# Turning the third token group by transposing transfers instead of TensorE, with w3's last tile loaded once

## The chip, the cores and the metric

The kernel runs on one core of a Trainium2 chip. The metric is the device time of one execution in microseconds, lower is better. The engines are named as in the profile: PE (TensorE's matmuls; PEld is its weight loads), DVE (VectorE), ACT (ScalarE), POOL (GpSimd) and SP (SyncE, which here issues nearly every DMA). "L453" is line 453 of the kernel.

## The reference

The input `x` has 2048 tokens of 448 channels. Two branches are added to it:

```python
xn  = layernorm(x)
out = x + A(xn) + B(xn)

def A(x):                      # spectral filter
    X = rfft2(x) * (w_r + 1j * w_i)
    return irfft2(X)

def B(x):                      # token shift, then MLP
    h  = gelu(layernorm(x) @ w1)                # w1: 448 x 448
    hs = concat(shift(h[:, 0:112], +1), shift(h[:, 112:224], -1),
                shift(h[:, 224:336], +2), shift(h[:, 336:448], -2)) @ w2
    x1 = x + hs
    h2 = gelu(layernorm(x1) @ w3) @ w4          # w3: 448 x 1792, w4: 1792 x 448
    return x1 + h2
```

## The kernel before

**Numbers.** Every matrix product is made in float16 from operands that are split into a high and a low half (`hi`, `lo = x - hi`), in three passes: hi·hi, lo·hi, hi·lo. The products with 448 channels contract over four tiles of 128, 128, 128 and 64 channels; the last, half-filled tile holds the high half in rows 0 to 63 and the low half in rows 64 to 127, so a split `x` has seven tiles (`xT`, 7 x 512 columns). For the same reason the last 64 rows of `w3` stand twice in `w3raw[:, 3]`, in partitions 0 to 63 and 64 to 127. The weights are scaled before splitting by a power of two that is found on chip: ACT squares and sums the raw weights (`squares`, L239), and `powers` (L245) adds the sums on DVE, adds them over the partitions by a small float32 matmul with ones (L254, "the power matmul") and makes the scale on DVE.

**Tokens.** Sixteen rows b of 128 tokens (token 16a + b stands in partition a of row b) form four groups, `GRP = [[14, 15, 0, 1], [2, 3, 4, 5], [6, 7, 8, 9], [10, 11, 12, 13]]`. "The third group" is group 2, rows 6 to 9. A shift of the tokens is then a change of row, so the w2 product of row b reads h of rows b-1, b+1, b-2 and b+2, one for each of the channel quarters k = 0 to 3.

**Stages of branch B, for each group.**

1. The group is normalised in place (`norm1`, L327).
2. It is turned, channels into partitions. Groups 0 to 2: 16 transposes by PE into PSUM (`turn_pe`, L398, L403), and from there a copy by ACT (L413) and a subtraction by DVE (L414) for each of four tiles make `xT` (`turn_copy`, `T1`). Group 3: `turn` (L819) splits each row into halves in SBUF first (ACT L825, DVE L826 and L827) and has SP transpose the row by one DMA (L828).
3. `w1_unit(g, i)` (L465) multiplies by w1 (L453, 11 matmuls for each row), applies the gelu on ACT (L474), splits the result into halves (ACT L475, DVE L476) and has SP transpose it into `hT` (L479), one DMA for each row.
4. `w2_mm(b, ks)` (L485) makes the w2 product of row b for the channel quarters `ks`, three matmuls for each (L497), and `w2_tile` finishes a row and adds it to x (DVE L504).
5. `ln2` (L507) normalises again and transposes by DMA into `x2all`, which lies in the memory `x2mem`.

The MLP follows: `front` (L424: w3; the gelu; halves in `hf`) and `back` (L772: w4) for 8 groups of 256 tokens and 7 pairs of feature tiles. It runs in the order of low priority, as filler between everything else; branch A (the transforms) is interleaved with it. `w3_split` (L831) makes the halves of w3 in eight pieces, four for each half of the features.

**Order of the work.** The program is written in the order of priority. A scheduler with a model of the times builds each engine's queue from that: of the instructions that are ready in its model, the one of highest priority goes next. `with behind(key)` adds an edge: what is issued inside comes behind the named instructions in the queue of the same engine. It is an order and no wait. Each engine, SP too, works off its queue in order. The keys in this change: `("a2")` the copies that turn group 2, `("a3")` the same for group 3, `(g, i)` the two halves of h of a unit, `("h", g, i)` its transposing DMA, `("w2", b)` the last w2 matmul issued for row b, `("p3")` the power matmul of w3, `("T", g)` the PE transposes of a group.

**Memory.** `bank(tag, ...)` gives one of two PSUM banks for each of the four tags mm, acc, tr and sp; a new user waits until the bank's last one has been read. `stage(name, n, side)` gives one of two SBUF buffers: side 0 holds first w1 and later ln2's rows 0 and 1, side 1 holds w2, then group 3's halves.

Of the kernel before, what the change touches and what calls it, by code (L numbers as in the profile page):

```python
# [13 lines left out]
F16 = mybir.dt.float16  # L14
I32 = mybir.dt.int32
AF = mybir.ActivationFunctionType
ALU = mybir.AluOpType
# [17 lines left out]
PIN = [("a3",), ("a3",), ("a3",), ("a3",)]  # L35
WMAX = [(1, 4), (1, 5), (1, 6), (2, 0), (2, 1), (2, 2), (2, 3), (2, 4)]
LATE = [(2, 2), (2, 3), (2, 4), (2, 5)]
# [84 lines left out]
def body(tc, nc, x, wf, w1, w2, w3, w4, c_g, c_n, c_small, out):  # L122
# [89 lines left out]
    def load_w3(ts):  # L212
        for t in ts:
            if t < 3:
                SY.dma_start(w3raw[:, t], w3[128 * t:128 * t + 128])
            else:
                for h in range(2):
                    SY.dma_start(w3raw[64 * h:64 * h + 64, 3], w3[384:448])

    load_w3([0, 1])  # L220
    load_x(3)
    load_w3([2])
    x2mem = pw.tile([128, 9 * F], F16, name="x2mem")
# [20 lines left out]

    def powers(m, n, key, tag="acc", mid=None):  # L245

        t = pc.tile([128, 1], F32, name=f"pt{key}")
        i = V.tensor_reduce(out=t, in_=m[:, :n + 1], axis=AX.X, op=ALU.add)
        after["t" + key] = (i.ins,)
        if mid:  # L250
            with behind("t" + key):
                mid()
        pm = bank(tag, f"pm{key}") if isinstance(tag, str) else tag
        i = T.matmul(pm[:, 0:1], ones, t, start=True, stop=True)  # L254
        after["p" + key] = (i.ins,)
        e = pc.tile([128, 3], I32, name=f"pe{key}")
        V.tensor_scalar(out=e[:, 0:1], in0=pm.bitcast(I32)[:, 0:1], scalar1=1, scalar2=0x7F800000,
                        op0=ALU.logical_shift_right, op1=ALU.bitwise_and)
        V.tensor_scalar(out=e[:, 1:2], in0=e[:, 0:1], scalar1=-1, scalar2=185 << 23, op0=ALU.mult, op1=ALU.add)
        i = V.tensor_scalar(out=e[:, 2:3], in0=e[:, 0:1], scalar1=1, scalar2=69 << 23, op0=ALU.mult, op1=ALU.add)  # L260
        after["s" + key] = (i.ins,)
        return e.bitcast(F32)[:, 1:2], e.bitcast(F32)[:, 2:3]
# [202 lines left out]
    def w1_unit(g, i, pm=None):  # L465
        if pm is None:
            pm = bank(("tr" if g == 1 else "mm", "acc")[i // 2], f"pw1_{g}{i}")
            w1_in(g, [(i, pm)], range(4))
        c = CS[GRP[g][i]]
        pm = pm[:, :D]  # L470
        pv_ = pm.rearrange("p (k n) -> p k n", k=4)
        h = hs_buf[c % (HS if g == 3 else HS + 2)]
        with behind(0, i - 2) if g == 0 and i > 1 else contextlib.nullcontext():
            A.activation(out=pm, in_=pm, func=AF.Gelu_apprx_tanh, scale=gsc[:, c:c + 1])  # L474
        u = A.activation(out=h[:, 0, :, 0:112], in_=pv_, func=AF.Copy, scale=h1)  # L475
        v = V.scalar_tensor_tensor(out=h[:, 1, :, 0:112], in0=pv_, scalar=h1, in1=h[:, 0, :, 0:112],  # L476
                                   op0=ALU.mult, op1=ALU.subtract)
        o = h_at(g, i)
        d = SY.dma_start_transpose(out=hT[g][:, :, o:o + 128], in_=h.rearrange("p i k n -> p (i k n)"))  # L479
        after[g, i] = u.ins, v.ins  # L480
        after["h", g, i] = (d.ins,)
# [3 lines left out]
    def w2_mm(b, ks):  # L485
        if b not in w2b:
            w2b[b] = bank("sp", f"pw2_{b}")
        for k in ks:
# [330 lines left out]
    def turn(g):  # L819

        xTs[g] = p1.tile([128, 7, 512], F16, tag="xT", bufs=2, name=f"xT{g}")
        y = stage(f"x{g}", 8 * D, 1, F16).rearrange("p (i n) -> p i n", i=4)
        for i, b in enumerate(GRP[g]):
# [4 lines left out]
            d = SY.dma_start_transpose(out=xTs[g][:, :, 128 * i:128 * i + 128], in_=h)  # L828
        after["t", g], after[f"a{g}"] = (d.ins,), (u.ins, v.ins)

# [85 lines left out]
    h_alloc(1)  # L916
    for k in range(4):
        w1_unit(1, k)
    for b in range(2):
        w2_mm(b, (2, 0))  # L920
    after["T", 2] = after["w2", 1]
    T1(2)
    with behind("h", 1, 3):
        load_w3([3])
    with behind("w2p"):
        n1[0][2]()
        n1[1][2]()
        for f in n1[2][:3]:
            f()
    for b in range(2):  # L930
        with behind("T", 2):
            w2_tile(b, (1, 3))
# [3 lines left out]
    with behind("w2", 1):  # L936
        for k in range(4):
            w1_unit(2, k)
    for k in range(4):
        with behind(*(("a2",), ("a2",), (2, 0), (2, 1))[k]):  # L940
            squares(m3[:, k:k + 1], w3raw[:, k])
    s3, r3 = powers(m3, 4, "3", "mm")
    h3 = pc.tile([128, 1], F32, name="h3")
    V.tensor_scalar(out=h3, in0=s3, scalar1=2.0 ** -5, scalar2=None, op0=ALU.mult)
    for b in range(2, 4):
        w2_tile(b)
    turn(3)
# [6 lines left out]
    for b in range(4, 8):  # L954
        w2_tile(b)
        with behind(*PIN[b - 4]):
            w3_split(2 * b - 8)
            w3_split(2 * b - 7)
            for i in (2 * b - 10, 2 * b - 9):
                if i >= 0:  # L960
                    squares(m4[:, i:i + 1], flat(w4raw[:, 2 * i:2 * i + 2]), junk4)
# [114 lines left out]
```

## Time and profile before

| | |
|---|---|
| median of 3 runs | 413.18 us (413.17 to 413.48) |
| the profiled execution's own time | 413.19 us |
| its span, first to last instruction | 411.4 us |
| PE busy | 406.0 us (99%) |
| DVE, ACT, POOL busy | 294.4, 247.7, 114.6 us |
| granted TensorE clock | 0.999 |
| PE transposes (L403) | 48 in all, 16 for the third group, from 33.01 to 34.76 us |
| group 3's transposing transfers (L828) | 4, landing 3.0 us after issue (median) |

The profile is of one execution. In a timeline row the columns are the start in us, how long it took in us, the engine, the line, the operation, what is written and read, the shape and the number of instructions merged into the row; in square brackets, if at all, the idle time before and what ended it. Matmuls overlap, so the time of a run of matmuls is read from its start to the start of the next one. A row of the groups has the busy time in us and the mean of one in ns behind the bar. In the windows, each stretch has the PE, PEld, DVE, ACT and POOL busy time, then the clock, the busy share of the DMA engines and the GB/s that they moved.

### The profile page before, as it was taken

Reading aid. Unit: us, or ns where it says so; the run is one execution under the profiler, and the core shown is the slowest. Engines: PE = TensorE matmul, PEld = TensorE weight load, DVE = VectorE, ACT = ScalarE, POOL = GpSimd, SP = SyncE. Lnnn points to the kernel's source line nnn. Section 1 sums busy time; section 2 is a strip of 40 time slices with the busy share of each in tenths; the row PEclk is TensorE's granted clock in tenths of the full one; section 3 lists DMA queues with packets and bytes.
Section 4 is the critical chain, followed back from the end, with each engine's and each line's share of the span. In section 5 each row is a group of like instructions: output and inputs, shape, how many; then the busy total and the mean of one; then the engine's idle time right before and its main releaser. Section 6 shows DMA issues by size and latency. Waiting matters only on the chain.

```text
span 411.4 us, 8535 instructions
## 1 busy us (share of the span) xinstructions
PE 406.0 (99%) x3314; PEld 290.1 (71%) x3314; DVE 294.4 (72%) x638; ACT 247.7 (60%) x427; POOL 114.6 (28%) x205
## 2 busy tenths in 40 slices
PE   8999999999999999999999999999999999999996
PEld 3655555666667877776887888777776776677885
DVE  5988999897644758863689889875776787667122
ACT  4697979964638766862678888873343434342321
POOL 2987810011217746400031121211212221121000
PEclk9999999999999999999999999999999999999999
DMA  8979499806811383437056655610000213233001
GB/s 279 365 219 202 96 175 324 192 2 142 173 47 45 91 274 132 120 84 165 13 141 178 154 142 143 170 56 2 2 0 2 69 50 107 69 94 130 24 0 46
DMA packets 53496, 48.53 MB, mean 118 GB/s; under 512 B 37600, under 2 KB 48480, under 8 KB 53456
## 3 DMA queue, kind: packets, MB, share of 16 engines
q1 hardware_dynamic: 53456, 47.99, 43.5%
q8 instruction: 26, 0.43, 0.4%
q14 instruction: 14, 0.11, 0.1%
HBM read 35.52 MB, written 3.67 MB: 95 GB/s over the span
## 4 chain that ended last, share of the span: by engine, by line
PE 93%; DVE 3%; DMA 2%; ACT 1%; POOL 1%; issue 0%
PE pw L424 33%; PE acc L772 31%; PE pw L497 8%; PE pw L453 6%; PE pu L693 3%; PE ps L590 3%; PE pp L647 2%; PE pe L713 2%; PE px L664 2%; PE py L735 2%; DMA h<-x2mem 1%; DMA xt<-x 1%; DVE sta L312 1%; PE pta L403 1%; DVE xT L414 0%; DVE xt L352 0%
## 5 line engine op out<-in xcount | busy, mean ns | idle before, releaser
L424 PE MATMUL pw<-x2mem,w3p 128*128 128x256 f16 x1232 | 149.6, 273 | 0.0
L772 PE MATMUL acc<-w4p,hf 128*128 128x448 f16 (+1 forms) x714 | 138.0, 341 | 0.0
L424 PEld LDWEIGHTS <-w3p 128*128 128x128 f16 x1232 | 118.6, 98 | 19.4
L772 PEld LDWEIGHTS <-hf 128*128 128x128 f16 x714 | 69.4, 98 | 48.3 <-DVE hf L753 0.3
L749 ACT ACTIVATE pw<-pw,pe 128x512 f32<-128x512 f32 x56 | 36.7, 656 | 64.6 <-PE pw L424 63.4
L753 DVE SCALAR_TENSOR_TENSOR hf<-pw,h,hf 128x512 f16<-128x512 f32 x56 | 41.9, 749 | 43.6 <-ACT hf L752 43.3
L497 PE MATMUL pw<-w2p,h 112*128 112x448 f16 x192 | 39.4, 352 | 0.1
L752 ACT ACTIVATE hf<-pw,h 128x512 f16<-128x512 f32 x56 | 38.4, 685 | 1.2
L674 POOL TENSOR_TENSOR z<-te 128x450 f32<-128x450 f32 x16 | 16.0, 1003 | 73.0 <-DVE te L672 69.2
L453 PE MATMUL pw<-w1p,xT 128*128 128x448 f16 x176 | 35.1, 352 | 0.3 <-ACT xT L413 0.3
L720 POOL TENSOR_TENSOR e<-e 128x226 f32<-128x226 f32 x16 | 11.5, 721 | 77.8 <-ACT e L717 74.6
L497 PEld LDWEIGHTS <-h 112*128 112x128 f16 x192 | 18.6, 98 | 16.2 <-DMA h<-x2mem 0.5
L453 PEld LDWEIGHTS <-xT 128*128 128x128 f16 x176 | 17.1, 99 | 15.9 <-ACT xT L413 0.5
L654 ACT ACTIVATE pf<-pp 64x450 f16<-64x450 f32 x32 | 17.4, 543 | 16.7 <-DVE pf L655 8.3
L717 ACT ACTIVATE e<-pe 128x452 f32<-128x452 f32 x16 | 8.8, 548 | 26.4 <-PE pe L713 26.4
L655 DVE TENSOR_TENSOR pf<-pp,pf 64x450 f16<-64x450 f32 x32 | 19.9, 622 | 5.9 <-ACT pf L654 5.6
L570 POOL TENSOR_TENSOR xr<-xf 128x452 f32<-128x452 f32 x8 | 8.9, 1115 | 32.0 <-issue 27.6
L669 ACT ACTIVATE te<-px 64x450 f32<-64x450 f32 x32 | 17.3, 539 | 0.5
L728 DVE TENSOR_TENSOR vh<-e,vh 128x448 f16<-128x448 f32 x16 | 10.0, 625 | 9.7 <-ACT vh L727 9.7
L573 POOL TENSOR_TENSOR f<-xr 128x452 f32<-128x452 f32 x16 | 16.1, 1030 | 0.6
L581 DVE TENSOR_TENSOR xh<-f,xh 128x452 f16<-128x452 f32 x16 | 12.7, 833 | 5.0 <-ACT xh L580 5.0
L722 DVE TENSOR_TENSOR e<-e 128x113 f32<-128x113 f32 x16 | 9.9, 618 | 7.8 <-POOL e L720 7.8
(172 smaller groups left out, 600.5 us busy)
## 6 DMA issues: line engine op xcount, KB each, us to landing
wc<-wf SPq DMA_DIRECT2D x32, 225.0 KB, 3.6
wl<-wf SPq DMA_DIRECT2D x8, 450.0 KB, 3.7
xf<-x SPq DMA_DIRECT2D x8, 448.0 KB, 3.4
xt<-x SPq DMA_DIRECT2D x3, 896.0 KB, 11.1
w3raw<-w SPq DMA_DIRECT2D x3, 896.0 KB, 14.6
xr<-x SPq DMA_DIRECT2D x12, 224.0 KB, 2.6
out<-xr SPq DMA_DIRECT2D x12, 224.0 KB, 1.9
gn<-c_g SPq DMA_DIRECT2D x16, 128.0 KB, 3.2
```

Of the source, the lines that this page charges most:

```text
L424: T.matmul(ps_out, wp[:, wi + t, cols], xT[:, xi + t, tok], start=t == 0 and wi + xi == 0, stop=t == 3 and wi == 4)
L453: m = T.matmul(pm[:, :D], xTs[g][:, xi + t, 128 * i:128 * i + 128], w1p[:, wi + t], start=t == 0 and p == 0, stop=t == 3 and p == 2)
L497: m = T.matmul(w2b[b][:, :D], hT[g][:112, 4 * hi + k, o:o + 128], w2p[:, wi, k], start=k == 2 and hi + wi == 0, stop=k == 3 and hi == 1)
L573: P.tensor_tensor(out=f[:, :, k:k + 2].rearrange("p b s d -> p s b d"), in0=u[:, :, 0], in1=u[:, :, 1], op=op)
L654: A.activation(out=hi, in_=src, func=AF.Copy)
L655: V.tensor_tensor(out=lo, in0=src, in1=hi, op=ALU.subtract)
L669: i = A.activation(out=e[64 * h:64 * h + 64], in_=px_[64 - 64 * h:128 - 64 * h, :2 * DF], func=AF.Copy)
L674: P.tensor_tensor(out=z, in0=t[:, 0], in1=t[:, 1], op=ALU.add)
L749: A.activation(out=pm, in_=pm, func=AF.Gelu_apprx_tanh, scale=r3)
L752: i = A.activation(out=h[:, 0], in_=pm, func=AF.Copy, scale=h3)
L753: j = V.scalar_tensor_tensor(out=h[:, 1], in0=pm, scalar=h3, in1=h[:, 0], op0=ALU.mult, op1=ALU.subtract)
L772: m = T.matmul(to, h[:, hi, o:o + 128], w4p[0][:, wi, f, r], start=f == 0 and n == 0, stop=f == 13 and n == 2)
```

## The change

- Group 2 is turned as group 3 is: `turn(2)` stands between the first and the second w1 unit of group 1, and the 16 PE transposes with their copies are gone. Its halves use stage side 0. The halves of the units (1, 2) and (1, 3) come behind its copies on ACT and DVE.
- Of the w2 products, rows 0, 1, 2 (quarters 2 and 0) and row 3 (quarter 2) now stand ahead of the rest. PSUM: the w1 units of group 2 use tags tr and acc, the w2 products of rows 2 and 3 use mm, and the power matmul uses sp.
- w3's last 64 rows are loaded once, right behind the third tile in the opening loads; a second DMA, in SP's queue behind the transposition of h of unit (2, 0), copies them on chip to partitions 64 to 127.
- The squares of w3 come earlier: three behind the halves of unit (1, 3), the fourth behind those of unit (2, 0), the fourth on 64 partitions only. The power matmul is put right behind the last w1 matmul of group 2, and the rest of rows 2 and 3 of the w2 product behind it.
- `w3_split` also comes behind the halves of unit (2, 3). One of branch A's eight maxima (`WMAX`, used at L605) moves behind another piece of the MLP.

```diff
-WMAX = [(1, 4), (1, 5), (1, 6), (2, 0), (2, 1), (2, 2), (2, 3), (2, 4)]
+WMAX = [(1, 4), (1, 5), (2, 0), (2, 0), (2, 1), (2, 2), (2, 3), (2, 4)]
...
             else:
-                for h in range(2):
-                    SY.dma_start(w3raw[64 * h:64 * h + 64, 3], w3[384:448])
+                SY.dma_start(w3raw[0:64, 3], w3[384:448])
 
     load_w3([0, 1])
     load_x(3)
-    load_w3([2])
+    load_w3([2, 3])
...
-    def powers(m, n, key, tag="acc", mid=None):
+    def powers(m, n, key, tag="acc", mid=None, pin=None):
...
-        i = T.matmul(pm[:, 0:1], ones, t, start=True, stop=True)
+        with behind(*pin) if pin else contextlib.nullcontext():
+            i = T.matmul(pm[:, 0:1], ones, t, start=True, stop=True)
...
     def w1_unit(g, i, pm=None):
         if pm is None:
-            pm = bank(("tr" if g == 1 else "mm", "acc")[i // 2], f"pw1_{g}{i}")
-            w1_in(g, [(i, pm)], range(4))
+            pm = bank(("tr" if g < 3 else "mm", "acc")[i // 2], f"pw1_{g}{i}")
+            after["u", g, i] = (w1_in(g, [(i, pm)], range(4)).ins,)
...
-        u = A.activation(out=h[:, 0, :, 0:112], in_=pv_, func=AF.Copy, scale=h1)
-        v = V.scalar_tensor_tensor(out=h[:, 1, :, 0:112], in0=pv_, scalar=h1, in1=h[:, 0, :, 0:112],
-                                   op0=ALU.mult, op1=ALU.subtract)
+        with behind("a2") if g == 1 and i > 1 else contextlib.nullcontext():
+            u = A.activation(out=h[:, 0, :, 0:112], in_=pv_, func=AF.Copy, scale=h1)
+            v = V.scalar_tensor_tensor(out=h[:, 1, :, 0:112], in0=pv_, scalar=h1, in1=h[:, 0, :, 0:112],
+                                       op0=ALU.mult, op1=ALU.subtract)
...
         if b not in w2b:
-            w2b[b] = bank("sp", f"pw2_{b}")
+            w2b[b] = bank("mm" if b in (2, 3) else "sp", f"pw2_{b}")
...
-        y = stage(f"x{g}", 8 * D, 1, F16).rearrange("p (i n) -> p i n", i=4)
+        y = stage(f"x{g}", 8 * D, g - 2, F16).rearrange("p (i n) -> p i n", i=4)
+        done = ()
...
-        after["t", g], after[f"a{g}"] = (d.ins,), (u.ins, v.ins)
+            done += (u.ins, v.ins)
+        after["t", g], after[f"a{g}"] = (d.ins,), done
...
-    for k in range(4):
+    w1_unit(1, 0)
+    turn(2)
+    for k in range(1, 4):
         w1_unit(1, k)
-    for b in range(2):
-        w2_mm(b, (2, 0))
-    after["T", 2] = after["w2", 1]
-    T1(2)
-    with behind("h", 1, 3):
-        load_w3([3])
+    for b, ks in ((0, (2, 0)), (1, (2, 0)), (2, (2, 0)), (3, (2,))):
+        w2_mm(b, ks)
...
-    for b in range(2):
-        with behind("T", 2):
+    with behind("w2", 3):
+        for b in range(2):
             w2_tile(b, (1, 3))
...
+    with behind("h", 2, 0):
+        SY.dma_start(w3raw[64:128, 3], w3raw[0:64, 3])
     for k in range(4):
-        with behind(*(("a2",), ("a2",), (2, 0), (2, 1))[k]):
-            squares(m3[:, k:k + 1], w3raw[:, k])
-    s3, r3 = powers(m3, 4, "3", "mm")
+        n = 128 if k < 3 else 64
+        with behind(*((1, 3), (1, 3), (1, 3), (2, 0))[k]):
+            squares(m3[:n, k:k + 1], w3raw[:n, k])
+    s3, r3 = powers(m3, 4, "3", "sp", pin=("u", 2, 3))
...
-    for b in range(2, 4):
-        w2_tile(b)
+    with behind("p3"):
+        w2_tile(2, (1, 3))
+    w2_tile(3, (0, 1, 3))
...
-        with behind(*PIN[b - 4]):
+        with behind(*PIN[b - 4]), behind(2, 3):
```

## Prediction

> **What bounds the kernel now.** I read the page's busy shares, clock and chain first, then the waits of PE.
>
> ```profile
> PE 406.0 (99%) x3314; PEld 290.1 (71%) x3314; DVE 294.4 (72%) x638; ACT 247.7 (60%) x427; POOL 114.6 (28%) x205
> PEclk9999999999999999999999999999999999999999
> PE 93%; DVE 3%; DMA 2%; ACT 1%; POOL 1%; issue 0%
> PE wps L808 <- DVE wsrc L186: 1.2, 1, 1.2
> PE wps L846 <- DVE xt L352: 0.5, 1, 0.5
> PE pw L453 <- ACT xT L413: 0.3, 1, 0.3
> ```
>
> PE is busy 406.0 of 411.4 us at full clock, and its three listed waits come to 2.0 us, all before 12 us. So the kernel is one long PE queue: whatever leaves that queue shortens the run, and whatever makes PE wait lengthens it, one for one. The next view is therefore PE's timeline around the third group.
>
> ```profile
> 30.74 2.44 PE L497 MATMUL pw<-w2p,h 112*128 112x448 f16 x12
> 33.01 1.91 PE L403 MATMUL pta<-ident,xt 128*128 128x128 f32 x16
> 34.76 2.68 PE L497 MATMUL pw<-w2p,h 112*128 112x448 f16 x12
> 37.28 8.49 PE L453 MATMUL pw<-w1p,xT 128*128 128x448 f16 x44
> 45.61 6.98 PE L497 MATMUL pw<-w2p,h 112*128 112x448 f16 x36
> 52.42 0.28 PE L254 MATMUL pm<-pt,ones 128*128 128x1 f32 x2
> 52.56 2.24 PE L453 MATMUL pw<-w1p,xT 128*128 128x448 f16 x11
> 54.64 2.44 PE L497 MATMUL pw<-w2p,h 112*128 112x448 f16 x12
> ```
>
> Matmuls overlap, so I cost them from start to start. Twelve w2 matmuls take 33.01 - 30.74 = 2.27 us, 0.189 each. The 16 transposes take 34.76 - 33.01 = 1.75 us. The second dozen takes 37.28 - 34.76 = 2.52 us, so 0.25 us of it is a wait. The 44 w1 matmuls take 8.33 us, 0.189 each.
>
> The last view is what SP issues in the same stretch, since the transposes go there.
>
> ```profile
> 25.97 4.08 SPq L479 DMA_TRANSPOSE h<-hs  x3
> 30.15 2.65 SPq L479 DMA_TRANSPOSE h<-x2mem  x2
> 32.89 1.29 SPq L479 DMA_TRANSPOSE h<-hs  x1
> 34.28 2.65 SPq L479 DMA_TRANSPOSE h<-hs  x2
> 36.98 1.22 SPq L218 DMA_DIRECT2D w3raw<-w  x2
> 43.34 1.24 SPq L479 DMA_TRANSPOSE h<-x2mem  x1
> 46.94 2.56 SPq L828 DMA_TRANSPOSE xT<-x  x2
> 54.67 2.65 SPq L479 DMA_TRANSPOSE h<-hs  x2
> h<-hs SPq DMA_TRANSPOSE x12, 3.3
> xT<-x SPq DMA_TRANSPOSE x4, 3.0
> 31.53 3.99 DMA h<-x2mem
> ```
>
> SP is full from 25.97 to 36.9 with the eight h rows of groups 0 and 1 (call them h00 to h13): five issues from 25.97 to 32.89 are 1.38 us apart. An issue lands 3.0 to 4.0 us later; 3.3 is the middle. PE is full, and behind it SP is nearly so: the change moves work from the one to the other.
>
> **The change, part by part.**
>
> *PE's transposes go.* Sixteen fall out: -1.75 us. The 0.25 us wait of the second dozen is also in play.
>
> *What PE does meanwhile.* The new order puts 21 w2 matmuls (k = 2, 0 of rows 0, 1, 2 and k = 2 of row 3) where 12 stood. It adds no work; 9 matmuls, 9 x 0.189 = 1.70 us, move ahead of the w1 matmuls of group 2 and are missing behind them. They use only h of group 0. The first that needs h03 is number 16, at 30.74 + 15 x 0.189 = 33.58; h03 is issued at 30.15 and lands at 33.45 (at 34.1 with the slowest landing: 0.5 us wait). Then the dozen with k = 1, 3: its fourth needs h10 at 30.74 + 24 x 0.189 = 35.28, and h10 landed at 31.53 + 3.99 = 35.52, a wait of 0.24 as before. The last three need h11 at 35.52 + 1.13 = 36.65; issued at 32.89, it lands at 36.2. The dozen ends at 37.22.
>
> *Four transposing transfers of x join SP's queue.* The rows that feed them:
>
> ```profile
> 30.64 0.79 ACT L349 ACTIVATE xt<-xt,nma,vy 128x448 f32<-128x448 f32 x1
> L825 ACT ACTIVATE x<-xt 128x448 f16<-128x448 f32 x4 | 2.3, 574 | 0.0
> L826 DVE TENSOR_TENSOR x<-xt,x 128x64 f16<-128x64 f32 x4 | 1.1, 266 | 0.2 <-ACT x L825 0.2
> L827 DVE TENSOR_TENSOR x<-xt,x 128x384 f16<-128x384 f32 x4 | 2.2, 559 | 0.0
> L413 ACT ACTIVATE xT<-pta 128x512 f16<-128x512 f32 (+1 forms) x12 | 6.5, 593 | 4.0 <-PE pta L403 4.0
> L414 DVE TENSOR_TENSOR xT<-pta,xT 128x512 f16<-128x512 f32 (+1 forms) x12 | 8.0, 684 | 0.8 <-ACT xT L413 0.7
> ```
>
> The last of the four rows of x is normalised at 31.43; a copy (0.57) and two subtractions (0.27 and 0.56) make a row ready by about 32.8, and the first rows earlier. ACT does 4 x 0.574 = 2.3 us instead of 4 x 0.593 = 2.4; DVE does 4 x (0.266 + 0.559) = 3.3 instead of 4 x 0.684 = 2.7. So SP's queue decides, not the data. Only h12 and h13 are pinned behind the copies of x; h10 goes first, and h11's pieces were ready before the last row of x was normalised. I take the order h10, h11, x, x, x, x, h12, h13. The first x then has the slot at 34.28 and lands at 37.3 (3.0), 37.6 (3.3) or 38.3 (3.99). I take 37.6: the queue is busy, so the h median fits better than that of the spaced x transfers. The others follow 1.38 apart (38.9, 40.3, 41.7), and PE needs them 2.08 apart (11 x 0.189): only the first can stall. h12 and h13 go out at 39.8 and 41.2 and land at 43.1 and 44.5; they are used after 46: no cost.
>
> So the w1 matmuls of group 2 start at 37.6, not 37.28, with 1.70 us more w2 work behind them: 37.6 - 37.28 - 1.70 = **-1.4 us**. Bounds: -0.7 (landing at 38.3), -1.7 (37.3), and -2.0 (1.75 + 0.25) if nothing waits.
>
> The Trainium skill speaks against this move: VectorE: DVE Perf Modes, "Rules for kernel authors", sends a 128x128 transpose to TensorE where a PSUM destination will do, and "The three transpose paths" prices it at 390 ns there and at 1309 ns by DMA. By it the 4 x 7 tiles would need 36.7 us of DMA (an estimate from that page), and the kernel would be some 30 us slower. The rows above disagree: one transfer of seven such tiles lands in 3.0 us.
>
> *w3's last tile.*
>
> ```profile
> 22.00:24.00 2.00, 2.00 (x13) 1.02 (x11) 1.92 (x6) 1.98 (x4) 1.90 (x5) 1.00 1.00 416
> 24.00:26.00 2.00, 2.00 (x11) 0.99 (x11) 1.97 (x7) 2.00 (x5) 1.92 (x4) 1.00 0.19 75
> w3raw<-w SPq DMA_DIRECT2D x2, 448.0 KB, 6.0
> ```
>
> The first load (448 KB) moves to the end of the opening loads. These run at 416 GB/s (last column) until about 24.4 (0.19 of the next 2 us), so it adds 1.1 us and ends at 25.5, still ahead of the first transpose at 25.97. Price nothing; without that gap, h00 would be up to 1.1 us later, and it has 30.74 - 29.3 = 1.4 to spare. The second load becomes a copy on chip behind h20 (43.34). It may share the DMA with the x transfer at 46.94: up to 1.0 us more landing (3.99 against 3.0). That row lands at 49.9 and is needed at 52.56 - 1.4 = 51.2, so it is covered. SP issues one transfer fewer there (-0.6). Nothing to nothing; I take 0.
>
> *Squares of w3 and the power matmul.* The power matmul (L254) moves from 52.42 to right behind the last w1 matmul of group 2 (37.6 + 8.33 = 45.9), and w2 tiles 2 and 3 queue behind it, so PE now stands on it.
>
> ```profile
> 35.58 1.70 ACT L243 ACTIVATE xr<-w3raw 128x1792 f16<-128x1792 f32 x1
> 37.40 1.70 ACT L243 ACTIVATE xr<-w3raw 128x1792 f16<-128x1792 f32 x1
> 41.32 0.61 ACT L474 ACTIVATE pw<-pw,gsc 128x448 f32<-128x448 f32 x1 [2.13 <-issue]
> ```
>
> ACT finished group 2's copies at about 35.6 before and has the same load now, so the squares run at 1.82 us each from 35.6: three end at 41.1; the gelu and copy of row (2, 0) take 1.2, the fourth square 1.8: 44.1, plus some 0.5 for DVE's sum: 44.6. Margin 1.3 us. Price 0; if that cover is gone, up to 1.6 us (three more ACT instructions of 0.6 ahead, and DVE late by 1.1).
>
> *PSUM tags and pins.* Group 2's w1 units take the banks that group 1's gave up by about 36, w2 rows 2 and 3 those of group 0's first units: free long before. The moved maximum (L265) only swaps order on DVE, for which PE has no wait. Price 0.
>
> *What is late next.* PE comes 1.4 us earlier to the rows of h and x behind.
>
> ```profile
> 60.13 0.73 PE L497 MATMUL pw<-w2p,h 112*128 112x448 f16 x3
> ```
>
> The tightest is h22: issued at 54.67, landed at 58.0, used at 60.13: 2.1 us to spare, more than the shift. From 67.7 PE has front matmuls as filler. So the gain should reach the end. Sum against the profiled run's own 413.19 (span 411.4; the shown median is 413.18): 413.2 - 1.4 = **411.8**.
>
> **Rivals.**
>
> *A, slower: SP's queue becomes the bound.* All four x transfers go ahead of h11 on SP, while PE's order keeps the last three matmuls of w2 row 1, which need h11, ahead of group 2's w1. h11 is then issued at 32.89 + 4 x 1.38 = 38.4 and lands at 41.7; PE needs it at 36.65 and waits 5.1 us instead of the listed 0.35 (37.22 to 37.57). That makes -1.4 - 0.35 + 5.1 = +3.3: 416.5. It decides from two x transfers ahead of h11 (landing 39.0; the start of w1 at 39.6 is +0.6). For it: turn(2) stands ahead of unit (1, 1) in the program, and SP is the fuller queue. Against: h11's data are ready first, and PE may run w1 matmuls of group 2 in between. The row PEclk shows full clock throughout; no run here shows a stall of that length. The Trainium skill, TensorE: Matmul & The Clock Gate, "What's actually happening", halves the clock after about 3.4 us of idling, which would add up to 1.7 us here (an estimate from that page).
>
> *B, no change: PE waits elsewhere.* The power matmul is late by its full 1.6 us (ACT takes gelus and copies first), or h22 slips by 2 us because DVE, which does 0.6 us more, is behind. 411.8 + 1.6 = 413.4. For it: PE's order there is fixed and DVE is close to full. Against: the margins of 1.3 and 2.1 us.
>
> *C, the whole gain:* PE finds w1 or w2 work for every wait: 411.2. This lies on the forecast's side.
>
> That the change doesn't do what it says isn't a rival of its own: the 16 transposes are gone by the diff, and the price of what replaces them is A and B.
>
> **How the numbers follow.** About 0.2%, 0.83 us, is what a measurement of this kernel can tell from no change. Forecast 0.52 (411.2 to 412.4, by the landings) and C 0.10 are faster: 0.62. B 0.14: same. A 0.15, and 0.09 for a milder form of A or two waits of B together (+0.9 to +2.0): slower 0.24. The range leaves out A's full price and a little below C: 411.0 to 414.8. The forecast's own range is 411.2 to 412.5.
>
> **What would show it.** After: no L403 rows past 23 us; seven or eight L497 triples in one run from 30.7; four L828 rows on SP starting near 34.3; the L453 run of group 2 starting at 37.2 to 38.3 with a wait on a DMA of xT of at most 1 us; L254 near 45.9 without a wait; L497 row 60.13 near 58.7. Wrong if PE's waits list an h or xT transfer with over 1.4 us, or L254 with a wait on DVE, or if the busy time of PE falls by 1.8 us and the span doesn't.

## The result, and the profile after

The changed kernel takes 413.90 us (median of 22 executions, 412.99 to 415.0), the kernel before 413.19 us (22 executions, 412.96 to 413.79). The ratio is 1.0016, with a 95% interval of 1.0010 to 1.0023: a little slower, where 411.8 us was forecast. The profiled execution took 413.97 us; its span is 412.1 us, 0.7 more than before.

The page of the kernel after, its busy line, clock and chain:

```profile
PE 404.7 (98%) x3298; PEld 287.9 (70%) x3298; DVE 295.0 (72%) x642; ACT 247.4 (60%) x427; POOL 118.6 (29%) x205
PEclk9999999999999999999999999999999999999999
PE 81%; DMA 5%; DVE 4%; ACT 3%; POOL 3%; issue 2%; SPq 1%; ACTq 0%; POOLq 0%; DVEq 0%
```

PE is busy 1.3 us less, with 16 instructions fewer, and the span is longer. So PE waits more. PE's share of the chain fell from 93% to 81%, because the chain, followed back from the end, now leaves PE at one of its new waits (76.92 us) and runs from there over DVE, ACT and the first of w4's loads. The waits of PE (engine, line, releaser; total us, times, longest):

```profile
PE pw L498 <- DMA h<-hs: 1.1, 1, 1.1
PE pw L498 <- DVE xt L505: 0.5, 1, 0.5
PE wps L849 <- DVE nma L342: 0.4, 1, 0.4
```

The first two are new and are not where the change is made. PE's timeline and one row of SP's around the third group, and the windows' row from 24 to 26 us:

```profile
31.12 7.32 PE L498 MATMUL pw<-w2p,h 112*128 112x448 f16 x36
38.28 8.49 PE L453 MATMUL pw<-w1p,xT 128*128 128x448 f16 x44
47.36 0.28 PE L254 MATMUL pm<-pt,ones 128*128 128x1 f32 x2
35.11 5.25 SPq L830 DMA_TRANSPOSE xT<-x  x4
24.00:26.00 2.00, 2.00 (x11) 0.90 (x10) 1.97 (x6) 2.00 (x5) 1.92 (x5) 1.00 1.07 272
```

Here the change does what it was forecast to do. The 16 transposes are gone, 36 w2 matmuls run in one piece, and the w1 matmuls of group 2 follow at 38.28 without a wait for the first x transfer, which was issued at 35.11 and landed 3.1 us later, at 38.2. Before, w1 started at 37.28 with 24 w2 matmuls done; 12 more are worth 2.27 us, so PE is ahead by 37.28 + 2.27 - 38.28 = 1.27 us. It stays ahead by 1.28 us until the first front matmul (66.43 against 67.71 before, the same matmuls done). Then PE's timeline from 66 us, after, and rows of the same stretch of before:

```profile
66.43 2.35 PE L424 MATMUL pw<-x2mem,w3p 128*128 128x256 f16 x20
68.61 1.87 PE L498 MATMUL pw<-w2p,h 112*128 112x448 f16 x9
70.32 0.49 PE L424 MATMUL pw<-x2mem,w3p 128*128 128x256 f16 x3
70.77 0.54 PE L498 MATMUL pw<-w2p,h 112*128 112x448 f16 x2
72.41 2.44 PE L498 MATMUL pw<-w2p,h 112*128 112x448 f16 x12 [1.11 <-DMA h<-hs]
74.69 0.28 PE L254 MATMUL pm<-pt,ones 128*128 128x1 f32 x2
75.02 1.36 PE L424 MATMUL pw<-x2mem,w3p 128*128 128x256 f16 x11
76.92 2.43 PE L498 MATMUL pw<-w2p,h 112*128 112x448 f16 x12 [0.53 <-DVE xt L505]
```

```profile
69.52 2.13 PE L424 MATMUL pw<-x2mem,w3p 128*128 128x256 f16 x18
71.49 1.30 PE L497 MATMUL pw<-w2p,h 112*128 112x448 f16 x6
72.95 1.30 PE L497 MATMUL pw<-w2p,h 112*128 112x448 f16 x6
72.92 0.90 PEld L497 LDWEIGHTS <-h 112*128 112x128 f16 x6
74.86 0.73 PE L497 MATMUL pw<-w2p,h 112*128 112x448 f16 x3
79.53 0.28 PE L254 MATMUL pm<-pt,ones 128*128 128x1 f32 x2
```

From start to start, the first wait is 72.41 - 70.77 - 2 x 0.189 = 1.26 us, the second 76.92 - 75.02 - 11 x 0.109 = 0.70 us (0.109 is a front matmul's pitch). Their sum, 1.97, is the 1.28 that PE was ahead and the 0.7 by which the run is longer. Nothing else differs later: from 82 us to the end each run has only the same two waits of over 0.1 us, 0.11 near 193 us and 0.15 near 248.

The first wait is row 8's quarter k = 3, which reads h30 (group 3's first row, row 10; some expectations below call it "h's last row of group 2"). The second is row 10's PSUM bank, which is free once DVE has added row 8 (L505). What these two hang on, from the timelines of SP, ACT and DVE after (columns as before), with the landing times of the h transfers from 60 to 80 us:

```profile
59.87 2.32 SPq L228 DMA_DIRECT2D x2mem<-w  x4
65.22 7.38 SPq L480 DMA_TRANSPOSE h<-hs  x3
DMA to landing us min/median/max: 3.0/4.9/7.1
72.70 0.62 ACT L476 ACTIVATE hs<-pw,h 128x448 f16<-128x448 f32 x1
73.36 0.68 DVE L477 SCALAR_TENSOR_TENSOR hs<-pw,h,hs 128x448 f16<-128x448 f32 x1 [1.39 <-ACT hs L476]
74.28 0.16 DVE L247 TENSOR_REDUCE pt<-m 128x1 f32<-128x8 f32 x1
76.19 0.67 DVE L505 SCALAR_TENSOR_TENSOR xt<-xt,cs,pw 128x448 f32<-128x448 f32 x1
```

The whole of w4 (3.2 MB in four loads) stands on SP's queue at 59.87, ahead of h30 at 65.22. h30 is the transfer that takes 7.1 us to land, at 72.4. Before, it was issued at 68.06 and landed 4.8 us later, at 72.9:

```profile
68.06 5.09 SPq L479 DMA_TRANSPOSE h<-hs  x3
DMA to landing us min/median/max: 3.1/3.7/4.8
```

In both kernels that is about 1 us behind the last of w4's loads, which was issued at 61.44 and landed at 71.4 after, and was issued at 61.66 and landed at 72.0 before.

Before, h30 was already as late as PE could bear. Of the 24 w2 matmuls of rows 8 and 9, nine stand ahead of 69.52 (row 8's other quarters) and six at 71.49 (row 9's quarters 2 and 0); the six at 72.95 (row 8's k = 3 and row 9's k = 1) are those that read h30, and the three at 74.86 read h31. The first weights of the six are loaded at 72.92 and h30 landed at 72.88, so its margin was under 0.1 us.

ACT, after, reaches the halves of group 3's last row, h33, at 72.70, since w4's seven squares stand between; DVE idles for that, and row 8's addition stands behind it in DVE's order, at 76.19.

### The profile page after: what moved, and what is told of

Same layout as the page of the kernel before. It is cut to its first block, busy times and chain, and to the rows that moved or that the text cites. A ratio compares the mean times of both kernels' runs of the same rounds, so it can differ in the third digit from the quotient of the medians.

```text
span 412.1 us, 8520 instructions
## 1 busy us (share of the span) xinstructions
PE 404.7 (98%) x3298; PEld 287.9 (70%) x3298; DVE 295.0 (72%) x642; ACT 247.4 (60%) x427; POOL 118.6 (29%) x205
## 4 chain that ended last, share of the span: by engine, by line
PE 81%; DMA 5%; DVE 4%; ACT 3%; POOL 3%; issue 2%; SPq 1%; ACTq 0%; POOLq 0%; DVEq 0%
PE pw L424 32%; PE acc L773 31%; PE pw L498 3%; PE pu L694 3%; PE ps L591 3%; PE pp L648 2%; PE pe L714 2%; PE px L665 2%; PE py L736 2%; ACT xr L242 2%; DMA w1s<-w 1%; DMA x2mem<-w 1%; DMA h<-hs 1%; DMA xT<-x 1%; DVE x L829 1%
## 5 line engine op out<-in xcount | busy, mean ns | idle before, releaser
L773 PEld LDWEIGHTS <-hf 128*128 128x128 f16 x714 | 69.4, 98 | 48.3 <-DVE hf L754 0.4
L675 POOL TENSOR_TENSOR z<-te 128x450 f32<-128x450 f32 x16 | 16.0, 1002 | 73.0 <-DVE te L673 69.2
```

Of the source, the lines that this page charges most:

```text
L675: P.tensor_tensor(out=z, in0=t[:, 0], in1=t[:, 1], op=ALU.add)
L773: m = T.matmul(to, h[:, hi, o:o + 128], w4p[0][:, wi, f, r], start=f == 0 and n == 0, stop=f == 13 and n == 2)
```

## Experiments

Two theories at first. *W*: from 66 to 82 us the run is paced by w4's load, its squares on ACT and what stands behind them; PE only arrives earlier. *O*: the fixed order of PE and DVE is to blame; it puts waiting instructions ahead of ready ones, and another order gets the gain. "Us" is the median; ratios are to the kernel before, timed on the same chip beside it, with 95% intervals. Waits are PE's, from start to start, in one profiled execution.

### Moving one obstacle out of the way

**e1_filler_first.** PE's order: the last w2 matmuls of rows 8 and 9 behind the second front.

```diff
-    for b in range(8, 12):
+    w2_mm(8, (2, 0, 1))
+    with behind("fm", 0, 1):     # the second front's last matmul
+        w2_tile(8, (3,))
+    w2_mm(9, (2, 0))
+    with behind("fm", 0, 1):
+        w2_tile(9, (1, 3))
+    for b in range(10, 12):
         w2_tile(b)
```

> The changed kernel, with one edge in PE's order: the matmuls of w2 rows 8 and 9 that read group 3's h come behind the last front matmul (L424) of the second feature pair, so that some 21 filler matmuls (2.3 us) stand ahead of them. Theory O (PE's order: the filler stands behind the waiting matmul): the wait of 1.27 us at 71.2 us goes, and the 0.70 us at 76.2 us at least in part; 411.9 to 412.6 us against 413.9 of the changed kernel. Theory W (the load of w4 holds everything that follows, whatever PE does meanwhile): the waits move to a later place and the time stays at 413.7 to 414.0.

414.24 us, 1.0025 [1.0015, 1.0035]. The wait for h30 is gone, but the waits from 66 to 82 us come to 2.76, most of it at w4's power matmul:

```profile
PE pm L254 <- DVE pt L247: 1.6, 1, 1.6
PE pw L499 <- DVE xt L506: 0.7, 2, 0.5
```

**e2_half_w4.** Only the first two of w4's four loads are left, 1.8 of its 3.2 MB (1.4 MB are left out, where the expectation has 1.5); what reads the other part reads these a second time, and the seven squares stay.

```diff
-        for i in range(4):
+        for i in range(2):
             load_w4(i)
```

> The changed kernel without the last two of the four loads of w4 (1.5 of 3.2 MB left out; the first loads' values stand in for them). Theory W: the transposes of h of group 3 land about 3.3 us after their issue at 65 us instead of 7.1, PE waits for none of them, and the sum of w4's squares comes earlier, so both waits go: 411.9 us. Theory O: PE stands in the same order, and at least 0.7 us of wait stays: 412.7 to 413.9.

414.61 us, 1.0034 [1.0022, 1.0046]. h30 now lands 4.5 us after its issue and PE doesn't wait for it. Waits of 1.16, 1.25 and 1.01 us (DVE's additions, the power matmul) take its place; ACT's squares still run to 75.0. So the load isn't the only obstacle.

**e6_w4_part_early.** The first quarter of w4 ten microseconds earlier.

```diff
+    with behind("h", 2, 1):
+        load_w4(0)
...
-        for i in range(4):
+        for i in range(1, 4):
             load_w4(i)
```

> The changed kernel with the first of the four loads of w4 moved ahead on SP, behind the transposition of h of unit (2, 1) at 50.4 us instead of 59.9. Theory W: ACT, which stood idle from 60.9 to 65.25 us for this load, squares the first part 4 us earlier, the sum of the squares is ready by about 72 instead of 74.3, h of group 3 lands 2 us earlier, and the waits fall from 1.97 to under 0.7 us: 412.0 to 412.7. Theory O: with the order as it is at least 1.2 us stay: 413.2 to 414.

414.71 us, 1.0045 [1.0028, 1.0062]. Waits: 0.89 at 57.0, for group 3's xT that the early load delays, then again h30 (1.29), the power matmul (0.64) and an addition (0.44).

**e5_filler_and_power.** e1's order, and w4's power matmul behind the third front.

```diff
+    with prio(FILL):
+        for n in range(3):
+            front(0, n, ("mm", "tr")[n % 2])
-    s4, r4 = powers(m4, 7, "4")
+    s4, r4 = powers(m4, 7, "4", pin=("fm", 0, 2))
```

> The order of PE of the filler experiment, and the power matmul of w4 behind the last of 66 filler matmuls (front of the third feature pair) as well; nothing else moves. Theory O (PE's fixed order puts matmuls that wait for w4's load and its squares ahead of ready filler): all waits over 0.3 us between 66 and 82 us go, 2.0 us in sum, and the time is 411.9 to 412.3. Theory W (w4's load and the seven squares behind it set the pace whatever PE's order is): the waits come back behind it, at the bank of a w2 row or at w4's halves, and the time stays at 413.5 to 414.3.

415.7 us, 1.0056 [1.0037, 1.0074], spread from 413.59 to 417.44; the profile is of the fastest execution. In six of the ten executions (415.65 us and more) the mean granted clock was 0.996, in the other four (413.59 to 415.75) 1.00; the profile has no part of that loss, and what lowered the clock is open. There one wait is left, 2.24 us at 77.26, the addition of row 8 on DVE, 2.7 us later than in the kernel after.

**e9_rows_then_power** and **e11_rows_later.** As e5, with DVE's sum of the squares behind the additions of rows 8 and 9, and with row 8's last matmuls behind the first front (e9) or half of the second (e11), row 9's behind half of the second (e9) or the whole (e11).

```diff
+    for b, ks in ((8, (2, 0, 1)), (9, (2, 0))):
+        w2_mm(b, ks)
+        with behind(*(("fm", 0, 0), ("fh", 0, 1))[b - 8]):
+            w2_tile(b, (3,) if b == 8 else (1, 3))
+    with behind("x1", 9):
+        s4, r4 = powers(m4, 7, "4", pin=("fm", 0, 2))
```

> The kernel after, with TensorE's and VectorE's order changed together between 60 and 82 us: the first three fronts of the first group come first; the last w2 matmuls of row 8 stand behind the first front, those of row 9 behind half of the second, the power matmul of w4 behind the third, and VectorE's sum of w4's squares behind the first residual adds of rows 8 and 9. Every instruction of the kernel after is still there. Theory O (the time is lost to a fixed order, in which waiting matmuls and adds stand ahead of ready ones): the three obstacles of the runs so far (h's last row of group 2, w4's squares, row 8's add on VectorE) each have ready work in front, so that of the 1.97 us that TensorE waits here in the kernel after under 0.7 us is left, and the time is 411.9 to 412.7. Theory W (the stretch is paced by w4's load, its seven squares and what hangs on them, whatever the order): the waits come back in another place, 1.5 us or more in sum between 60 and 95 us, and the time is 413.5 to 415.

> As the run with the rows ahead of the power matmul, but row 8's last w2 matmuls stand behind half of the second front and row 9's behind the whole of it: some 16 matmuls, 3 us, later each. Theory O: h's last row of group 2 has landed for certain by then, but the adds and what follows them come 3 us later: waits under 1 us in sum between 60 and 82 us and 412 to 413, within 0.5 us of the other order. Theory W: waits of 1.5 us or more in sum at another place between 60 and 95 us, 413.5 to 415.

415.14 us, 1.0040 [1.0025, 1.0055], and 414.11 us, 1.0016 [1.0006, 1.0026]. Both have the wait for row 8's addition again: 2.14 us at 77.4 and 1.84 at 77.1, the latter with 0.46 and 0.43 for other additions. In e9 that addition runs at 78.97, though row 8's last matmul began 4.7 us before. Part of e9's time is not PE's order: in its profiled execution the clock was at half in the opening (0.50 in the row of the windows below), and group 2's w1 started at 39.2 instead of 38.3.

```profile
12.00:14.00 2.00, 2.00 (x9) 1.38 (x7) 2.00 (x5) 0.81 (x2) 1.87 (x4) 0.50 1.03 251
```

Theory O, in the form that PE's order alone decides, falls: five orders (after, e1, e5, e9, e11), and each time 2.0 to 2.8 us of waits between 66 and 87 us. Nor do W's times hold: e1, e2, e5 and e6 all came out above the ranges that the two theories had given.

### Parts of the change by themselves

**e4_pe_turn.** The kernel after, with group 2 turned by PE again (group 1's halves not pinned, the turn's PSUM banks from tags tr and acc).

```diff
-    turn(2)
...
+        if b == 1:
+            after["T", 2] = after["w2", 1]
+            T1(2)
```

> The changed kernel, but group 2 is turned by PE again (16 transposes behind the first twelve w2 matmuls); w3's last tile, the squares, the power matmul and the tags stay as changed. Theory W: PE comes to group 3's rows about 1.75 us later, no wait over 0.3 us is left there, and the time is before's plus the opening's 0.4: 413.5 to 413.7. If the transposing transfers themselves cost the time (theory T), it falls to 413.2 or below.

417.36 us, 1.0101 [1.0087, 1.0114], where 413.5 to 413.7 was expected. Waits from 74 to 93 us: 0.93 (for h30), 0.88, 0.49 and, at the first matmuls of w4, 1.74. Three of the four are in new places, so the run doesn't decide between the theories.

**e3_w3_twice.** The kernel after, with w3's last rows loaded twice from HBM behind h13, as before.

```diff
-    load_w3([2, 3])
+    load_w3([2])
...
-    with behind("h", 2, 0):
-        SY.dma_start(w3raw[64:128, 3], w3raw[0:64, 3])
+    with behind("h", 1, 3):
+        load_w3([3])
```

> The changed kernel, but w3's last rows are loaded twice from memory as before, behind h of the last unit of group 1; all else as changed. The first transposes of h should again land after 3.6 us (4.9 and 4.3 in the changed kernel) and PE should reach the w1 matmuls of group 2 0.2 to 0.5 us earlier. Theory W: the landing behind w4's load is fixed, so what PE gains early it waits later: 413.7 to 414.0. Theory R (the loss is the opening loads and whatever it shifts): 413.4 to 413.5 or less.

416.82 us, 1.0090 [1.0076, 1.0103]. The pinned power matmul waits; its row in the waits and in PE's timeline, the matmuls behind it, and two rows of the windows:

```profile
PE pm L255 <- DVE pt L248: 3.3, 1, 3.3
50.80 0.59 PE L255 MATMUL pm<-pt,ones 128*128 128x1 f32 x2 [3.26 <-DVE pt L248]
51.25 6.38 PE L499 MATMUL pw<-w2p,h 112*128 112x448 f16 x18
52.00:54.00 2.00, 2.00 (x7) 0.86 (x6) 1.96 (x6) 2.00 (x5) 0.00 (x0) 0.50 1.02 202
58.00:60.00 2.00, 2.00 (x13) 1.05 (x11) 2.00 (x3) 2.00 (x3) 0.00 (x0) 1.00 0.84 160
```

The clock that the throttle grants is 0.50 after that wait, and the 18 matmuls take 57.46 - 51.25 = 6.21 us instead of 3.40. No wait is left after 66 us: PE arrives too late for one. Like e4, this run and the next missed what either theory expected.

**e8_turn_alone.** The turn by transfers and the early w2 matmuls, but w3's load, squares and power matmul as before the change.

```diff
-    s3, r3 = powers(m3, 4, "3", "sp", pin=("u", 2, 3))
+    s3, r3 = powers(m3, 4, "3", "sp")
...
-    with behind("p3"):
-        w2_tile(2, (1, 3))
+    w2_tile(2, (1, 3))
```

> The changed kernel's transposing transfers and its order of the first w2 products, but w3's last tile loaded twice as before, the squares of w3 at their old places and the power matmul of w3 without its pin. Theory W: PE reaches 66 us 1.3 to 1.9 us earlier than before and loses most of it between 66 and 82 us: 413.0 to 414.0. Theory Q (the early squares and the pinned power matmul of w3 are what reorders the later work badly): 411.6 to 412.2.

418.38 us, 1.0125 [1.0111, 1.0139]. PE waits 4.23 us at 48.3 for group 3's xT, and runs on at half clock (0.50 from 52 to 58 us):

```profile
PE pw L454 <- DMA xT<-x: 4.1, 1, 4.1
```

So the two halves of the change need each other: with w3 loaded twice, the squares or the next transfers come too late for the new order. Why group 3's xT is late in e8 was not followed up.

**e7_before_4_transposes.** The kernel before with 4 of the 16 PE transposes; the other copies read the first bank.

```diff
+        if g == 2 and t:
+            return kept[0][:128 if t < 3 else 64]
```

> The kernel before, but group 2 is turned by 4 PE transposes instead of 16 (twelve left out, the other three tiles are copied from the first one's bank): PE has 1.31 us less to do at 33 us and nothing else of the change is made. Theory W: PE comes 1.3 us earlier to the stretch that w4's load paces; at least half of it is lost there: 412.5 to 413.2. Theory P (the loss is in the other parts of the change, not in PE's being early): 411.8 to 412.0.

414.37 us, 1.0028 [1.0018, 1.0039], where 411.8 to 413.2 was expected. Taking PE's work away and nothing else gains nothing: PE waits 1.50 us for h10 at 34.0 and 0.87 for h30 at 76.8.

```profile
PE pw L503 <- DMA h<-x2mem: 1.3, 1, 1.3
PE pw L503 <- DMA h<-hs: 0.7, 1, 0.7
```

### Finding the common cause

**e10_two_squares.** The kernel after with two of w4's seven squares.

```diff
-                if i >= 0:
+                if 0 <= i < 2:
                     squares(m4[:, i:i + 1], flat(w4raw[:, 2 * i:2 * i + 2]), junk4)
-    squares(m4[:, 6:7], flat(w4raw[:, 12:14]), junk4)
```

> The kernel after with two of the seven squares of w4 on ScalarE; the other five, some 6 us of ScalarE between 66 and 75 us, are left out (their sums are not formed). The loads and TensorE's order stay. If the two waits have two causes, as theory W has it, the transfer of h's last row behind w4's load and ScalarE's squares: the first wait (1.27 us at 70.95, on a DMA) stays at 1 to 1.4 us, the second (0.70 at 76.11, on VectorE's add of row 8) falls below 0.2, and the time is 413.1 to 413.5. If ScalarE's squares set both (a later chain to h's last row): both go, 412.0 to 412.6. If neither: as the kernel after, 413.7 to 414.3.

413.57 us, 1.0008 [0.9995, 1.0021]. The second wait fell to 0.21, as theory W has it; the first grew from 1.27 to 2.06, since PE came 0.84 us sooner to it (the same opening went faster in this execution, by 0.57 at group 2's w1). It ended at 72.36; in the kernel after, at 72.41. The transfer's landing doesn't move, and the first wait missed the expected 1 to 1.4.

**e12_both** has e1's and e10's edits together; **e13_before_two_squares** is the control, e10's edit in the kernel before.

> The edits of two earlier runs together: the last w2 matmuls of rows 8 and 9 behind the second front, and two of the seven squares of w4 (the other five are left out, their sums not formed). Alone, the first left waits of 2.8 us between 66 and 82 us in its profile (w4's power matmul, VectorE's adds), the second 2.3 (h's last row, landing at 72.3 whatever TensorE did). Theory W+O (the transfer behind w4's load and the chain of squares, reached through fixed queues, are all that the gain is lost to): both waits go, at most 0.6 us is left from 66 us on, and with the 1.3 us that TensorE is ahead at 66 us the time is 411.7 to 412.4. If a third wait takes their place, as in every run so far: 413 to 413.8.

> The kernel before with two of the seven squares of w4 (the other five are left out, their sums not formed): the control for the run with both edits. TensorE waits for nothing there from 36 us to 247 us, so by either theory the time stays at 412.9 to 413.4. If it falls by more, fewer squares are worth something by themselves, and that much of the other run's gain isn't the change's.

e13: 413.21 us, 0.9998 [0.9990, 1.0007]; the squares are worth nothing by themselves. e12: 413.9 us, 1.0022 [1.0009, 1.0035], and the expectation of 412 fails: one wait of 2.32 us at 78.0, for row 8's addition. But its trace shows what holds the others up. ACT's, DVE's and PE's rows, and the landing of the h transfers from 60 to 90 us:

```profile
72.51 0.63 ACT L477 ACTIVATE hs<-pw,h 128x448 f16<-128x448 f32 x1 [3.69 <-DMA h<-hs]
73.18 0.68 DVE L478 SCALAR_TENSOR_TENSOR hs<-pw,h,hs 128x448 f16<-128x448 f32 x1 [2.23 <-ACT hs L477]
79.72 0.67 DVE L506 SCALAR_TENSOR_TENSOR xt<-xt,cs,pw 128x448 f32<-128x448 f32 x1
80.44 4.70 PE L499 MATMUL pw<-w2p,h 112*128 112x448 f16 x24 [2.15 <-DVE xt L506]
DMA to landing us min/median/max: 3.0/5.1/7.7
```

ACT stands still for 3.69 us ahead of h33, with no square in between, until a transfer of h has landed. There are three staging buffers for group 3's four rows (`HS = 3`, `hs_buf[c % HS]`), so h33 takes h30's, and h30's transfer, behind w4's load, reads it until about 72.4. DVE waits for ACT, and its order has some 6 us of other work between that and row 8's addition. That makes theory *B*: w4's load ahead of h30 is behind both waits. The landing holds PE (row 8) and ACT (h33); with all seven squares ACT arrives at h33 no sooner than it lands, and the wait reads as one for the squares. The squares remain an obstacle of their own: taking away one of the two leaves the other at nearly the same time. ACT did h33 at 72.70 in the kernel after, and at 73.50 in e2, where h30 had landed at 69.2 and the squares alone were left.

**e14_half_load_too.** e12 and e2's half load together: the same order of PE up to w4's first matmuls, two squares, 1.8 of w4's 3.2 MB.

> The run with both edits, and w4's last two of four loads left out as well (1.5 of 3.2 MB; the splits read the first half twice, five of seven squares are left out). Theory B (one cause: h's first row of group 3 lands late, behind w4's load, and holds the staging buffer that ScalarE needs for the group's last row, and VectorE's order behind it): the row lands at 69 to 69.5 instead of 72.5, ScalarE's copy runs at about 70, VectorE's add of row 8 comes before 77, TensorE waits under 0.5 us in sum from 66 us on, and the time is 411.6 to 412.4. If VectorE's own order (two chains of small operations ahead of the add) sets the wait whatever lands when: about 2 us at 78 again and 413.3 to 414.

411.95 us, 0.9969 [0.9958, 0.9981]. PE has no wait over 0.2 us from 24 to 245 us. The rows that answer to those of e12:

```profile
68.66 0.63 ACT L477 ACTIVATE hs<-pw,h 128x448 f16<-128x448 f32 x1
77.13 0.68 DVE L506 SCALAR_TENSOR_TENSOR xt<-xt,cs,pw 128x448 f32<-128x448 f32 x1
77.88 4.71 PE L499 MATMUL pw<-w2p,h 112*128 112x448 f16 x24
DMA to landing us min/median/max: 3.1/3.4/3.9
```

The transfers land within 3.9 us of their issue instead of 7.7, ACT does h33 3.85 us sooner, DVE adds row 8 2.6 us sooner, and PE's wait is gone. Only the load differs from e12 (1.0022 against 0.9969), so with the order and the squares out of the way it was worth about 2.2 us. Against the control e13 the run is 1.2 us shorter by the ratios (0.9969 against 0.9998) and 411.03 - 409.57 = 1.46 us by the profiled spans: what PE had gained around the third group now reaches the end. The control leaves out the squares alone; no run halves w4's load in the kernel before, where PE has no wait at h30 that this could remove. No run has half the load and two squares in the PE order of the kernel after either, so what e1's order adds is open.

**e15_w4_in_two.** With all the work done: the last two of w4's loads behind h31 on SP, the last three squares behind h33 on ACT, and e1's order.

```diff
-        for i in range(4):
+        for i in range(2):
             load_w4(i)
...
         w1_unit(3, k)
+        if k == 1:
+            with behind("h", 3, 1):
+                for i in (2, 3):
+                    load_w4(i)
+    with behind(3, 3):
+        for i in range(4, 7):
+            squares(m4[:, i:i + 1], flat(w4raw[:, 2 * i:2 * i + 2]), junk4)
```

> The kernel after with all its work: the last two of w4's four loads stand on SyncE's queue behind the transfer of group 3's second row, the last three squares of w4 behind ScalarE's copy of group 3's last row, and the last w2 matmuls of rows 8 and 9 behind the second front of the first group. Theory B: the first row of group 3 lands at 69 to 70, the copies and adds no longer wait, w4's power matmul comes 6 us later at about 80 us with front matmuls in front: waits under 1 us in sum from 66 to 95 us, 411.9 to 412.9. If the later squares and the later split of w4 are what decides: a wait of 1.5 us or more at the power matmul or at the first matmul of w4 near 85 us, 413.5 to 415.

412.91 us (412.33 to 413.51), 0.9986 [0.9976, 0.9996]: faster than the kernel before by 0.5 us (413.39 beside it; 0.2 to 1.0 by the interval), and about 1 us faster than the changed one. SP's queue now has h30 and h31 between the loads, and PE's one wait of more than 0.2 us from 24 to 245 us is 0.66 at 77.6:

```profile
58.94 1.06 SPq L228 DMA_DIRECT2D x2mem<-w  x2
64.44 2.93 SPq L481 DMA_TRANSPOSE h<-hs  x2
67.42 1.06 SPq L228 DMA_DIRECT2D x2mem<-w  x2
78.36 2.43 PE L499 MATMUL pw<-w2p,h 112*128 112x448 f16 x12 [0.50 <-DVE xt L506]
```

**e16_row8_sooner**, e15 with row 8's last matmuls behind half of the second front, and **e17_before_w4_in_two**, e15's edits in the kernel before.

```diff
-    with behind("fm", 0, 1):
+    with behind("fh", 0, 1):
         w2_tile(8, (3,))
```

> The run with w4 in two parts, all work done, with row 8's last w2 matmuls behind half of the second front (about 72.5 us) instead of the whole of it (75 us). Theory B: group 3's first row has landed by 69 to 70, so nothing waits for it; VectorE's add of row 8 can come 2 us sooner, ahead of the splits of y, the wait of 0.66 goes to under 0.2, and the time is 412.0 to 412.7. If the add stays behind the splits, or a wait appears at another add: 412.8 to 413.5.

> The kernel before with the same edits as the run with w4 in two parts (w4's last two loads behind group 3's second row, three squares later, rows 8 and 9 behind the second front); all work done. TensorE waited for nothing there, so by theory B nothing is gained: 412.9 to 413.6, or more if the later power matmul waits. If it falls under 412.7, the two-part load is worth something without the change, and the other run's gain isn't the change's.

e16: 412.89 us, 0.9989 [0.9981, 0.9998], as e15. The wait for row 8's addition, now at 76.95, fell to 0.20, but waits of 0.80 and 0.53 for additions of other rows came up, so the expected 412.0 to 412.7 was missed. e17: 413.22 us, 1.0007 [0.9995, 1.0020], no wait of PE over 0.2 us between 24 and 247 us: the two-part load is worth nothing without the change. e15's gain is therefore the change's own, let through (0.9986 against 1.0007).

## Why the prediction was wrong, by its own steps

**The terms of the sum held, in part by luck.** The 16 transposes fell out for 1.75 us. The forecast of -1.4 at group 2's w1 matmuls measured -1.27. The wait for the first x transfer was 0 instead of 0.35, because PE ran 36 w2 matmuls ahead of w1 where 33 were reckoned; but x landed at 38.2 instead of 37.6, just ahead of PE, which was late itself. h11 was not held up (rival A's order didn't come about: the x transfers follow h11, from 35.11), and the power matmul of w3 ran at 47.36 without a wait.

**One price of nothing was 0.7 us in this execution.** w3's first load at the end of the opening loads was to be covered by h00's 1.4 us to spare. The DMA share from 24 to 26 us rose from 0.19 to 1.07, the first transposes of h landed 4.9 and 4.3 us after their issue instead of 3.6 and 3.3, and PE waited 0.19 us for the first and 0.29 for the second; PE had come to them 0.19 later. Together that took back what the missing waits (0.35 for x, 0.25 for h10) had given: the forecast's bound of -2.0 for no wait at all, and 0.7 on top, is the -1.3 that was measured. In the eleven other runs with this opening the first lands 3.4 to 4.7 us after its issue, PE waits at most 0.24 us here, and in all but e9 group 2's w1 starts at 37.7 to 38.1, a gain of 1.4 to 1.8 us. So the term was mis-sized by little, and by how much changes from one execution to the next.

**The step that failed is "what is late next".** It took the old order of PE, moved it 1.4 us forward and looked for the smallest margin, h22's 2.1 us; behind 67.7 it took the front matmuls for filler. Three things were wrong with it.

- The smallest margin was not h22's. Before, h30 landed at 72.88 and its weights were loaded at 72.92: under 0.1 us to spare, 12 us behind h22, where the step no longer looked. PE's 1.3 us had to become a wait there, since h30 landed only 0.5 us sooner (72.9 to 72.4).
- The queue was not only shifted but built anew. PE came to the matmuls that read h30 at 70.95 + 0.19 = 71.14 instead of 72.95, 1.8 us sooner: 1.28 is the gain, and the rest is the order, with 11 w2 and 23 front matmuls ahead of them since 66.43 where there had been 15 and 22 since 67.71. w4's power matmul came 4.8 us sooner. Filler helps only ahead of the waiting instruction: in e1, e5, e9 and e11, with filler there, PE's wait for h30 goes.
- The landing is set by w4's 3.2 MB, which the change doesn't move: in 17 of the 19 kernels h30 lands 0.7 to 1.1 us behind the last of w4's loads that were issued ahead of it (in e7 and e17 it was itself issued so late that it lands 1.8 and 2.8 us behind). e14 and e15 show that this load ahead of h30, with w4's squares, is what the gain was lost to: with both effects gone, on PE and on ACT and DVE, 411.95 us was measured, near the forecast's 411.8 (a kernel that leaves out part of w4); with the load and the squares only moved, 412.91.

Rival B ("PE waits elsewhere") was the right kind of case. It named the power matmul of w3 and h22 as the places; both were on time. The place was 12 us behind h22's use (58.7 by the forecast, 71.1), and it cost 1.97 instead of 1.6.

What stays open: why VectorE's order leaves 0.5 to 0.8 us of waits in e15 and e16, and what the best place for w4's second half is. A fourth staging buffer for h, which would take ACT's wait for h30 away by itself, was not tried, nor were the moved maximum and the PSUM tags undone by themselves.

## What to carry to other kernels

After taking work out of a full engine, go down its whole queue to the transfers that are not moved, and for each compare the landing with the first instruction that reads it: a kernel without a wait can still have a transfer with no margin, as h30 here. Where a scheduler rebuilds the queue, allow for more shift than the gain (for a gain of 1.3 us, 1.8 at h30 and 4.8 at w4's power matmul). Where several waits replace each other at the same time of the run, look for the transfer or buffer that lands then in all the runs, and split or delay the bulk load that stands ahead of it. Undo one thing at a time to find the places, but take two away together before calling a theory dead: here each single relief of the kernel after gained 0.3 us or nothing, and all of them together about 2 us, to 1.3 us under the kernel before.

## What the runs showed of the hardware

- A transposing transfer of one row lands 3.0 us after its issue when the DMA is quiet (L828 before), and 7.0 to 7.8 us when it is issued 3.0 to 4.3 us behind 3.2 MB of loads on the same queue (after, e1, e5, e9, e10, e11, e12); issued 6.4 us behind them, 4.8 (before, e13); behind the first 1.8 MB alone, 3.7 to 4.5 (e2, e14, e15, e16). In all of these it lands 0.7 to 1.1 us behind the last of the loads.
- PE waits of up to 2.3 us left the granted clock at 1.00 in the profiles of the kernel after, e2 and e12. Waits of 3.4 us (e3) and 4.2 us (e8) were followed by some 6 us at 0.50. This agrees in the main with the Trainium skill, TensorE: Matmul & The Clock Gate, "What's actually happening", which puts the limit at about 3.4 us of idling; no run here shows a wait between 2.3 and 3.4 us. Two traces don't fit a limit on the length of one wait: in e3 the clock is down (0.66 from 50.0 to 50.5 us) within 3 us of the end of PE's last matmul at 47.5, and in e9 it stands at 0.50 from 12 to 14 us though no wait of PE before it is longer than 1.3 us. Such a long wait costs nearly twice its length: e3's 3.4 us were followed by 2.8 us of slow matmuls.
